# Expert blocks woven between the steps of a DFT token mixer, with weights fetched per block

## The chip, the cores and the metric

One core of one Trainium2 chip runs the kernel. The metric is device time in microseconds (us) of one execution; lower is better. All data are float32 except two small bfloat16 matrices used for counting. Engines: PE = TensorE, DVE = VectorE, ACT = ScalarE, POOL = GpSimd, SP = SyncE, which here only issues DMAs.

## What is computed

```python
X = np.fft.fft(np.fft.fft(x, axis=1), axis=2).real      # x: 8 batches x 2496 tokens x 256
x = X.reshape(19968, 256)
logits = x @ w_gate                                      # 8 experts
expert_idx = np.argmax(logits, axis=1)
gate_w = softmax(logits)[arange, expert_idx]
for e in range(8):                                       # rows of expert e
    y[e's rows] = relu(x[e's rows] @ w1[e]) @ w2[e]      # 256 -> 1024 -> 256
out = gate_w[:, None] * y
```

Each token goes to one expert; the number of tokens per expert is known only at run time.

## The kernel before

The work stands in two parts, one behind the other.

**The transform, batch by batch.** `first(b)` reads batch b in four quarters. A quarter is two DMAs, `xl` (SP queue, L192) and `xh` (POOL, an indirect DMA, L193), which `fold` adds and folds on DVE (L201 to L211). PE multiplies the result (tile `s`), ACT copies it to `t1` (L227), and SP writes it to a scratch tensor `Td` (L228). `xl` and `xh` have two buffers each. `second(b, h)`, for each half h of a batch, reads `Td` back in another layout (`t4`, printed as `t`, L242) and does five groups g: two small matmuls (tile `p`, from `m` and `t`), a copy to `z` on ACT, two matmuls with `rd` (tile `p`, 273 columns), and copies into `rows` on ACT (L260) and DVE (L261). Then `route` finds each token's expert on DVE, counts ranks on PE (tile `rk`, 11 small matmuls), and POOL scatters ten groups of 128 rows to `Xs` in DRAM, one indirect DMA each (L158). `Xs` has one region per expert. Two weight DMAs of 1 MB (L146, L148) per batch bring all eight experts into SBUF for good.

**The experts.** After the last batch, POOL writes 16 groups of padding rows, DVE makes a table `tab` (expert and first row of each of 85 blocks of 256 rows), and the block loop runs. `load` (SP) reads the block's 256 rows `xb`; `turn` copies the expert's first weights to `wc` (DVE) and transposes `xb` on PE (tile `pt`); `layer1` is 16 matmuls into four `ph` tiles, each evacuated with ReLU into `hT` by ACT (L416) or DVE (L414) in turn; `layer2` is 16 matmuls into one tile `py`, whose halves t = 0 and 1 are scaled by ACT into `y` (L428) and scattered by POOL to the output (L158). Every float32 matmul is two passes of PE in the trace. The loop calls `layer1(i + 1)` before `layer2(i)`. In the transform the order of instructions is chosen by a scheduler; in the block loop it is the order of the code. Each engine executes its own list strictly in that order, and so does each DMA queue's issuing engine.

Of the kernel before, what the change touches and what calls it, by code (L numbers as in the profile page):

```python
# [12 lines left out]
I32 = mybir.dt.int32  # L13
# [14 lines left out]
BLK = 256  # L28
CAP = NT + BLK
NBLK = (NT + E * (BLK - 1)) // BLK  # L30
# [17 lines left out]
def shape_consts():  # L48
    """Tables of the transform and of the token numbering; they depend on the shapes alone."""
# [59 lines left out]

def block_consts():  # L110
    c = {
        "i": np.arange(NBLK),
        "i256": BLK * np.arange(NBLK),
        "e9": np.arange(E + 1),
        "low": (np.arange(E)[None, :] <= np.arange(E)[:, None]).reshape(-1),
        "cap": CAP * np.arange(E),
    }
# [8 lines left out]
def kernel(ctx: ExitStack, tc, x, w_gate, w1, w2, out):  # L126
# [12 lines left out]
    wp = ctx.enter_context(tc.tile_pool(name="wp", bufs=1))  # L139
    w1_sb = wp.tile([128, E, 2 * F], F32, name="w1_sb")  # L140
    w2_sb = wp.tile([128, E, FC * D], F32, name="w2_sb")
    ident = wp.tile([128, 128], F32, name="ident")
    tab = wp.tile([1, 2, NBLK], I32, name="tab")

    def load_weights(e):
        nc.sync.dma_start(out=w1_sb[:, e].rearrange("p (c f) -> p c f", c=2),  # L146
                          in_=w1[e].rearrange("(c p) f -> p c f", p=128))
        nc.sync.dma_start(out=w2_sb[:, e].rearrange("p (c d) -> p c d", c=FC),  # L148
                          in_=w2[e].rearrange("(c p) d -> p c d", p=128))

    # rows of Xs are written once each, before any block reads them
    def unordered(ins, group):
        ins = getattr(ins, "ins", ins)
        tc.declare_no_dep(ins, group=group, reason="no row is written twice")
        tc.add_to_no_dep_group(group, ins)

    def put_row(dst, idx, rows, last, group):
        unordered(pool.indirect_dma_start(  # L158
# [4 lines left out]
    with ExitStack() as keep, ExitStack() as mix:  # L163
        cp = keep.enter_context(tc.tile_pool(name="cp", bufs=1))
        xp = mix.enter_context(tc.tile_pool(name="xp", bufs=2))
        sp = mix.enter_context(tc.tile_pool(name="sp", bufs=2))
        ps1 = mix.enter_context(tc.tile_pool(name="ps1", bufs=2, space=PSUM))
        ps2 = mix.enter_context(tc.tile_pool(name="ps2", bufs=2, space=PSUM))
        ps3 = mix.enter_context(tc.tile_pool(name="ps3", bufs=2, space=PSUM))
        psr = mix.enter_context(tc.tile_pool(name="psr", bufs=2, space=PSUM))  # L170

        ix = cp.tile([NA, B * 4], I32, name="ix")
        at = (np.arange(B)[:, None] * (S // 4) + 7 - np.arange(4))[None]
        at = (at + 8 * (NA - 1 - np.arange(NA))[:, None, None]).reshape(NA, B * 4)
        nc.sync.dma_start(out=ix[:], in_=const_dram("ix", at.astype(np.int32)))

        con = {}
        for n, v in shape_consts().items():
            wide = (128, 2, NY + 2 * E) if n == "rd" else v.shape
            con[n] = t = cp.tile(list(wide), F32, name=n)  # L180
            act.dma_start(out=t[:, :, 0:NY] if n == "rd" else t[:], in_=const_dram(n, v))
        wg = cp.tile([128, 2, E], F32, name="wg")
        act.dma_start(out=wg[:], in_=w_gate.rearrange("(c p) e -> p c e", p=128))
        act.dma_start(out=ident[:], in_=const_dram("ident", np.eye(128, dtype=np.float32)))

        xrows = x.rearrange("b (n j) d -> (b n) (j d)", j=4)

        def load_x(b, q):
            xl = xp.tile([NA, 4, D], F32, tag="xl", name="xl")
            xh = xp.tile([NA, 4, D], F32, tag="xh", name="xh")  # L190
            src = x[b].rearrange("(p j) d -> p j d", j=NB)
            nc.sync.dma_start(out=xl[:], in_=src[:, 4 * q + 1:4 * q + 5])  # L192
            pool.indirect_dma_start(  # L193
                out=xh[:].rearrange("p j d -> p (j d)"), out_offset=None, in_=xrows,
                in_offset=bass.IndirectOffsetOnAxis(ap=ix[:, 4 * b + q:4 * b + q + 1], axis=0))
            return xl, xh

        def fold_d(o, a, n):
            """o = [a[d] + a[-d] for d in 0..128 | a[d] - a[-d] for d in 1..127], a[0] and a[128] once."""
            lo, hi = free(a, 1, [D, n], [1, H - 1]), free(a, D - 1, [D, n], [-1, H - 1])  # L200
            vec.tensor_tensor(free(o, 1, [D, n], [1, H - 1]), lo, hi, op=ALU.add)  # L201
            vec.tensor_tensor(free(o, H + 1, [D, n], [1, H - 1]), lo, hi, op=ALU.subtract)
            vec.tensor_copy(free(o, 0, [D, n], [H, 2]), free(a, 0, [D, n], [H, 2]))

        def fold(xl, xh, q):
            """The sum of x[s, d] and x[-s, -d], folded over d, in place of xh."""
            n = 3 if q == 3 else 4
            a, m = xl[:], xh[:]
            vec.tensor_tensor(free(a, 1, [D, n], [1, D - 1]), free(a, 1, [D, n], [1, D - 1]),
                              free(m, 3 * D + D - 1, [-D, n], [-1, D - 1]), op=ALU.add)  # L210
            vec.tensor_tensor(free(a, 0, [D, n]), free(a, 0, [D, n]), free(m, 3 * D, [-D, n]), op=ALU.add)  # L211
            fold_d(m, a, 4)
            return xh

        def stage1(b, q, pm, pm0):
            t1 = xp.tile([NR, 4, D], F32, tag="t1", name="t1")
            for half in range(2):
                ps = ps1.tile([NR, 2, D], F32, tag="s1", name="s1")
                for i in range(2):
                    s = 4 * q + 2 * half + i  # L220
                    if s < 15:
                        mm(ps[:, i], con["w1"][:, s], pm[:, 2 * half + i])
                        continue
                    for k, lo, hi in ((15, 0, H + 1), (17, H + 1, D)):
                        mm(ps[:, i, lo:hi], con["w1"][:, k], pm0[:, lo:hi], True, False)
                        mm(ps[:, i, lo:hi], con["w1"][:, k + 1], pm[:, 3, lo:hi], False, True)
                act.copy(t1[:, 2 * half:2 * half + 2], ps[:])  # L227
            nc.sync.dma_start(out=Td[b][:, 4 * q * D:4 * (q + 1) * D], in_=t1[:].rearrange("p j d -> p (j d)"))  # L228

        def first(b):  # L230
            x0 = xp.tile([NA, D], F32, tag="x0", name="x0")
            nc.sync.dma_start(out=x0[:], in_=x[b].rearrange("(p j) d -> p j d", j=NB)[:, 0])
            pm0 = xp.tile([NA, D], F32, tag="pm0", name="pm0")
# [86 lines left out]
        for b in range(B):  # L320
            if b + 1 < B:
                first(b + 1)
# [145 lines left out]
```

## Time and profile before

| | |
|---|---|
| median of 3 runs | 1748.61 us (1746.11 to 1749.07) |
| profiled execution, span | 1751.1 us |
| PE busy | 1500.2 us (86% of the span) |
| DVE, ACT, POOL busy | 463.7, 283.4, 381.4 us |
| first pass of the experts starts | 460.79 us |
| DMA moved | 127.45 MB, mean 73 GB/s |

The profiled execution's span lies 2.5 us above the median of the runs; the page lists no other time for it. "Granted clock" (PEclk) is the share of TensorE's full 2.4 GHz; its two levels are 1.2 and 2.4 GHz, so 0.70 is a mixture of the two. In a row of the timeline the first two numbers are the start and the length in us, and `[8.85 <-DVE oh L280]` means that the engine stood idle for 8.85 us just before it, until DVE had written `oh`.

### The profile page before, as it was taken

How to read it: one execution, taken by the hardware profiler on the slowest of the kernel's cores; microseconds unless marked ns; L12 is line 12 of the kernel's file. 1: busy time of each engine (PE TensorE's matmuls, PEld its weight loads, DVE VectorE, ACT ScalarE, POOL GpSimd, SP SyncE). 2: the span in 40 equal slices, each digit the busy share in tenths (PEclk: the TensorE clock that was granted, in tenths of full speed). 3: DMA queues.
4: the chain of work that ended last, by engine and by line, in shares of the span. 5: the costliest groups of instructions: out<-in, count | busy, mean ns of one | idle time of the engine just before them, and what ended most of it. 6: DMA issues, size and time to landing. Idle time of an engine off the chain costs nothing.

```text
span 1751.1 us, 20321 instructions
## 1 busy us (share of the span) xinstructions
PE 1500.2 (86%) x6940; PEld 1258.7 (72%) x6940; DVE 463.7 (26%) x1084; ACT 283.4 (16%) x581; POOL 381.4 (22%) x382
## 2 busy tenths in 40 slices
PE   3667776652599999999999999999999999999998
PEld 2445554542488888888888888888888888888886
DVE  3444443423222122222222212222222222222220
ACT  1222222221011111111111111111111111111111
POOL 1155554556211111111111111111111111111111
PEclk9987766776699999999999999999999999999999
DMA  8777766632211111101111111110111111111100
GB/s 212 207 246 213 216 198 197 191 108 79 76 37 37 36 33 37 36 29 34 37 34 33 37 37 37 35 37 28 35 37 34 37 35 37 36 37 37 29 18 0
DMA packets 62977, 127.45 MB, mean 73 GB/s; under 512 B 11612, under 2 KB 31696, under 8 KB 62880
## 3 DMA queue, kind: packets, MB, share of 16 engines
q1 hardware_dynamic: 40323, 71.35, 14.6%
q0 software_dynamic: 20192, 53.43, 9.2%
q10 hardware_dynamic: 2365, 1.38, 0.4%
q8 instruction: 61, 1.00, 0.3%
q14 instruction: 36, 0.29, 0.1%
HBM read 72.19 MB, written 56.28 MB: 73 GB/s over the span
## 4 chain that ended last, share of the span: by engine, by line
issue 65%; POOL 10%; PE 2%; DMA 1%; POOLq 1%; DVE 1%; ACT 0%; SPq 0%; DVEq 0%; ACTq 0%
POOL out_dram L158 9%; PE p L131 1%; POOL Xs L158 1%; POOLq L158 1%; DMA Xs<-rows,pi 0%; DMA Xs<-pad,ti 0%; ACT z L256 0%; DMA xb<-Xs 0%; PE rk L131 0%; DVE rows L261 0%; PE pr L131 0%; POOLq L463 0%; DVE eq L274 0%; DVE mx L273 0%; DVE eq L275 0%
## 5 line engine op out<-in xcount | busy, mean ns | idle before, releaser
L131 PE MATMUL py<-w_sb,hT 128*128 x2720 | 623.5, 382 | 48.0 <-ACT y L428 48.0
L131 PEld LDWEIGHTS py<-w_sb,hT 128*128 128x128 f32 x2720 | 509.8, 190 | 148.1 <-ACT y L428 82.2
L131 PE MATMUL ph<-xT,wc 128*128 128x256 f32 x2720 | 603.0, 380 | 0.0
L131 PEld LDWEIGHTS ph<-xT,wc 128*128 128x128 f32 x2720 | 511.6, 191 | 66.5
L158 POOL DMA_INDIRECT out_dram<-y,ro x170 | 165.2, 971 | 1127.7 <-ACT y L428 1118.1
L414 DVE TENSOR_SCALAR hT<-ph 128x512 f32<-128x512 f32 x170 | 117.5, 691 | 476.9 <-PE ph L131 476.9
L428 ACT ACTIVATE y<-py,xb 128x256 f32<-128x256 f32 x170 | 80.5, 473 | 712.1 <-PE py L131 712.1
L400 DVE COPY xT<-pt 128x512 f32<-128x512 f32 x85 | 58.7, 691 | 500.0 <-PE pt L398 500.0
L158 POOL DMA_INDIRECT Xs<-rows,pi x160 | 167.1, 1044 | 83.0 <-issue 61.8
L416 ACT ACTIVATE hT<-ph 128x512 f32<-128x512 f32 x170 | 101.5, 597 | 434.0 <-PE ph L131 386.0
L131 PE MATMUL s<-xh,w 78*80 78x256 f32 (+2 forms) x272 | 89.1, 475 | 54.0 <-issue 18.9
L131 PE MATMUL p<-rd,z 128*128 128x273 f32 x320 | 110.8, 497 | 13.7 <-DVE lg L262 9.3
L392 DVE COPY wc<-w_sb 128x2048 f32 x85 | 104.3, 1227 | 38.7 <-DMA Xs<-pad,ti 30.2
L131 PEld LDWEIGHTS s<-xh,w 78*80 78x80 f32 x272 | 49.5, 196 | 79.5 <-issue 54.2
L131 PEld LDWEIGHTS p<-rd,z 128*128 128x128 f32 x320 | 71.4, 237 | 41.3 <-ACT z L256 15.0
L398 PE MATMUL pt<-ident,xb 128*128 128x128 f32 x340 | 52.0, 276 | 41.1 <-DVE ro L394 41.1
L398 PEld LDWEIGHTS pt<-ident,xb 128*128 128x128 f32 x340 | 43.0, 143 | 49.9 <-issue 41.2
L131 PE MATMUL rk<-oh,tri 128*128 128x88 bf16 x16 | 3.8, 236 | 83.2 <-DVE oh L280 83.2
L131 PEld LDWEIGHTS <-ones 128*128 128x128 bf16 x160 | 8.4, 121 | 86.7 <-issue 86.6
L193 POOL DMA_INDIRECT xh<-in_x_dram,ix x32 | 33.4, 1043 | 146.9 <-PE s L131 71.9
L131 PEld LDWEIGHTS p<-m,t 128*128 128x128 f32 x320 | 55.5, 238 | 7.8 <-DVE t L247 2.8
L131 PE MATMUL p<-m,t 128*128 128x128 f32 x320 | 57.6, 325 | 1.8 <-DVE t L247 1.8
(75 smaller groups left out, 388.5 us busy)
## 6 DMA issues: line engine op xcount, KB each, us to landing
xb<-Xs SPq DMA_DIRECT2D x85, 258.0 KB
w_sb<-in_moe_w_dram SPq DMA_DIRECT2D x16, 1024.0 KB
Td<-t SPq DMA_DIRECT2D x32, 320.0 KB
t<-Td SPq DMA_DIRECT2D x16, 640.0 KB
xl<-in_x_dram SPq DMA_DIRECT2D x32, 312.0 KB
out_dram<-y,ro POOLq DMA_INDIRECT x170, 2.8
Xs<-rows,pi POOLq DMA_INDIRECT x160, 5.7
x<-in_x_dram SPq DMA_DIRECT2D x8, 78.0 KB
```

The costliest lines, as they stand in the source:

```text
L131: nc.tensor.matmul(o, lhsT=lhsT, rhs=rhs, start=start, stop=stop)
L158: unordered(pool.indirect_dma_start(out=dst, out_offset=bass.IndirectOffsetOnAxis(ap=idx, axis=0), in_=rows, in_offset=None, bounds_check= ...
L193: pool.indirect_dma_start(out=xh[:].rearrange("p j d -> p (j d)"), out_offset=None, in_=xrows, in_offset=bass.IndirectOffsetOnAxis(ap=ix[: ...
L392: vec.tensor_copy(wc[:], w1_sb[:, ds(ev, 1)])
L398: nc.tensor.transpose(pt[:, c, t], xb[:, t, c * 128:(c + 1) * 128], ident[:])
L400: vec.tensor_copy(xT[:], pt[:].rearrange("p c t k -> p c (t k)"))
L414: vec.tensor_scalar(o, ph[:], 0.0, None, op0=ALU.max)
L416: act.activation(o, ph[:], ACTF.Relu)
L428: act.activation(y[:, t], py[:, t], ACTF.Copy, scale=xb[:, t, D + 1:D + 2])
```

## The change

The two parts are merged. A batch's tokens are worked on by the experts while the next batch is transformed.

- `rounds()` fixes, from shapes alone, how many blocks can surely be filled after each batch: 2 blocks of 256 rows after batch 0, 6 of 256 after batch 1, 3 of 512 after batch 2, 5 of 512 after each of batches 3 to 7, and then 21 of 256 for what is left. That is 57 blocks and 21,760 rows, the same number of rows as 85 blocks of 256. `plan` makes a table on DVE for each of these groups at run time.
- `first` and `second` become generators that stop after each small step. `mixed(b)` alternates the steps of `first(b + 1)` and `second(b)`, 26 stops, and ends with the plan. A step of `second` does the first matmuls of group g and the second matmuls of group g - 1.
- `experts(todo)` is a generator too; it stops after each `ph` tile (counted 1) and each `py` tile (counted 2), 16 counts for a block of 512. The main loop gives `mixed` a number of steps for each count, so that all steps of a batch are used up in about four tenths of the counts of the round beside it (27 calls at 42 per 0.6 of a round).
- A block fetches its own `xb`, `w1` (1 MB) and `w2` (1 MB) by three SP DMAs, one block ahead, with two buffers of each. The resident weights, the `wc` copy and the weight index on PE are gone.
- The whole program is in the order of the code. `layer1` and `layer2` of a block follow each other; `py` is one tile of 128 rows with its own buffer; `hT` and `xT` have one buffer; PSUM is shared by both parts (`pm_` 3, `pst` 1, `psh` 2, `psy` 2 buffers).

```diff
-NBLK = (NT + E * (BLK - 1)) // BLK
+BIG, BLK = 512, 256
+TICKS = 42
-    w1_sb = wp.tile([128, E, 2 * F], F32, name="w1_sb")
-    w2_sb = wp.tile([128, E, FC * D], F32, name="w2_sb")
+    def fetch(b, size, tab, i):
+        n = size // 128
+        row = nc.sync.value_load(tab[:, 0, i:i + 1], min_val=0, max_val=ROWS - size)
+        ev = nc.sync.value_load(tab[:, 1, i:i + 1], min_val=0, max_val=E - 1)
+        xb = bp.tile([128, BIG // 128, W], F32, tag="xb", name="xb")
+        taken(nc.sync.dma_start(out=xb[:, 0:n].rearrange("p t c -> p (t c)"),
+                                in_=Xs[ds(row, size)].rearrange("(p t) c -> p (t c)", t=n)), b)
+        w1_sb = bp.tile([128, 2, F], F32, tag="w1", name="w1_sb")
+        nc.sync.dma_start(out=w1_sb[:], in_=w1[ds(ev, 1)].rearrange("o (c p) f -> p (o c) f", p=128))
+        w2_sb = bp.tile([128, FC, D], F32, tag="w2", name="w2_sb")
+        nc.sync.dma_start(out=w2_sb[:], in_=w2[ds(ev, 1)].rearrange("o (c p) d -> p (o c) d", p=128))
...
+            for f in range(FC // m):
+                ph = psh.tile([128, m, size], F32, tag="h", name="ph")
...
+                yield 1
+            if follow:
+                while follow[:3] not in tabs:
+                    yield 0
+                got = got or fetch_next()
+                turned = turn(follow[1], got[0])
+            y = bp.tile([128, BIG // 128, D], F32, tag="y", name="y")
+            for i in range(n):
+                py = psy.tile([128, D], F32, tag="y", name="py")
+                for f in range(FC):
+                    mm(py[:], hT[:, f, i * 128:(i + 1) * 128], w2_sb[:, f], f == 0, f == FC - 1)
+                act.activation(y[:, i], py[:], ACTF.Copy, scale=xb[:, i, D + 1:D + 2])
+                put_row(out, ro[:, i:i + 1], y[:, i], NT - 1, "out")
+                if i < n - 1 or n == 2:
+                    xT = next(turned, xT)
+                yield 2
...
+    for b in range(1, B):
+        side, done, due = mixed(b), 0, 0.0
+        total = 16 * sum(k * size for size, k, _ in rounds()[b - 1]) / BIG
+        while done < total:
+            w = next(work)
+            done += w
+            due += TICKS * w / (0.6 * total) if w else 1
+            while due >= 1:
+                next(side, None)
+                due -= 1
+        for _ in side:
+            pass
+    for _ in work:
+        pass
```

Where instructions stand on PE. Before, in the block loop (`pt` transposes, `ph` layer 1, then the reading of the expert's number and the first matmul of layer 2):

```order
L398 MATMUL pt<-ident,xb 128x128 x4
L131 MATMUL ph<-xT,wc 128x256 x16
L421 TENSOR_LOAD tab
L421 ISA x2
L131 ISA
L131 MATMUL py<-w_sb,hT 128x256
```

Now, in a block of 512 rows of the fifth round (`pr`, `p`, `s` are the transform's, `t_2600` a half of its batch):

```order
L162 MATMUL ph<-xT,w_sb 128x512 x10
L162 MATMUL pr<-t_2600,rot 128x5
L162 MATMUL ph<-xT,w_sb 128x512 x2
L162 MATMUL p_2914<-m_84,t_2600 128x128 x2
L162 MATMUL ph<-xT,w_sb 128x512 x2
L162 MATMUL p_2924<-m_84,t_2600 128x128 x2
L162 MATMUL p_2929<-rd,z 128x273 x2
L162 MATMUL ph<-xT,w_sb 128x512 x2
L162 MATMUL p_2939<-m_84,t_2600 128x128 x2
L162 MATMUL p_2944<-rd,z 128x273 x2
L162 MATMUL s_2951<-xh,w_82 80x256 x2
L162 MATMUL py<-w_sb,hT 128x256 x8
```

The transform's matmuls stand one step at a time between the block's, and no block starts with a reading of a number on PE any more.

On DVE, in the block loop before, one block (with what each instruction waits for):

```order
L392 COPY wc<-w_sb 128x2048 [waits DVE_49]
L394 CAST ro<-xb 128x2 [waits DMAHW0_49,DMASW3_49,DMASW2_49]
L400 COPY xT<-pt 128x512 [waits DVE_49,PE_49]
L414 TENSOR_SCALAR hT<-ph 128x512 [waits DVE_49,PE_49,Activation_49]
L414 TENSOR_SCALAR hT<-ph 128x512 [waits PE_49]
```

Now, in the same block of the fifth round:

```order
L490 TENSOR_SCALAR hT<-ph 128x512 [waits PE_49]
L240 TENSOR_TENSOR xl<-xl,xh 78x4x255 [waits DMAHW3_49,DMASW1_49]
L326 COPY rows<-p_2929 128x256 [waits DMASW4_49,DMASW5_49,DMASW2_49,DMASW7_49,DMASW0_49,Activation_49]
L327 COPY lg<-p_2929 128x16
L490 TENSOR_SCALAR hT<-ph 128x512 [waits PE_49]
```

A fold of the transform (L240), which waits for the two DMAs of its quarter, stands between two evacuations of the same block.

On SP, before, each block (a reading of its first row, and one DMA):

```order
L382 TENSOR_LOAD tab
L382 ISA x2
L384 ISA
L384 DMA xb<-Xs 128x516
```

Now, with a fetch of a block and what follows it in the fourth round:

```order
L439 DMA xb<-Xs 128x1032
L442 ISA
L442 DMA w_sb<-in_moe_w_dram 128x2x1024
L444 ISA
L444 DMA w_sb<-in_moe_w_dram 128x8x256
L298 DMA t_2139<-Td 128x5x256
L288 DMA Td<-t_2182 80x1024
L223 DMA xl<-in_x_dram 78x1024
```

The transform's reads and writes stand behind the two weight DMAs of a block on the same queue.

## Rows read from the trace of the kernel before

**Rows 1.** The page: PE's busy tenths and its granted clock in 40 slices.

```profile
PE   3667776652599999999999999999999999999998
PEclk9987766776699999999999999999999999999999
```

**Rows 2.** Busy time by stretch; then clock, DMA share, GB/s. Transform, then experts.

```profile
300.00:325.00 25.00, 17.48 (x72) 12.79 (x72) 10.85 (x39) 6.84 (x17) 14.03 (x13) 0.70 0.72 206
...
475.00:1735.00 1260.00, 1212.57 (x5677) 1041.06 (x5676) 279.06 (x413) 178.76 (x334) 162.24 (x167) 1.00 0.11 34
```

**Rows 3.** Timeline of PE: the start of the experts, and one later block.

```profile
460.79 1.57 PE L131 MATMUL ph<-xT,wc 128*128 128x256 f32 x3
...
1004.86 3.62 PE L131 MATMUL py<-w_sb,hT 128*128 x16
1009.04 3.72 PE L131 MATMUL py<-w_sb,hT 128*128 x16 [0.56 <-ACT y L428]
1012.60 0.60 PE L398 MATMUL pt<-ident,xb 128*128 128x128 f32 x4
1013.04 7.07 PE L131 MATMUL ph<-xT,wc 128*128 128x256 f32 x32
1019.95 3.62 PE L131 MATMUL py<-w_sb,hT 128*128 x16
...
1740.44 3.72 PE L131 MATMUL py<-w_sb,hT 128*128 x16 [0.61 <-ACT y L428]
```

**Rows 4.** Timeline of PE in the transform's second stage, at both clocks.

```profile
74.12 0.43 PE L131 MATMUL pr<-t,rot 128*128 128x5 f32 x2
74.41 2.06 PE L131 MATMUL p<-m,t 128*128 128x128 f32 x8
...
80.62 2.11 PE L131 MATMUL p<-rd,z 128*128 128x273 f32 x8
82.57 0.83 PE L131 MATMUL p<-m,t 128*128 128x128 f32 x6
...
84.94 3.22 PE L131 MATMUL s<-xh,w 78*80 78x256 f32 x14
88.00 0.20 PE L131 MATMUL rk<-oh,tri 128*128 128x88 bf16 x1
...
89.14 0.71 PE L131 MATMUL p<-m,t 128*128 128x128 f32 x4 [0.46 <-DVE t L247]
...
111.02 0.23 PE L131 MATMUL rk<-oh,tri 128*128 128x88 bf16 x1 [8.85 <-DVE oh L280]
```

**Rows 5.** Timeline of ACT and POOL: batch 0's last copy; scatters of batches 0 and 1.

```profile
42.71 0.58 ACT L227 COPY t<-s 80x512 f32<-80x512 f32 x1 [1.94 <-PE s L131]
...
90.34 1.01 POOL L158 DMA_INDIRECT Xs<-rows,pi  x1 [0.93 <-ACT z L256]
...
104.24 0.98 POOL L193 DMA_INDIRECT xh<-in_x_dram,ix  x1 [0.31 <-issue]
...
114.21 1.18 POOL L158 DMA_INDIRECT Xs<-rows,pi  x1 [0.32 <-issue]
...
159.42 1.19 POOL L158 DMA_INDIRECT Xs<-rows,pi  x1 [0.32 <-issue]
```

**Rows 6.** Between the parts: the last landing (chain); SP's first block loads.

```profile
452.10 3.12 DMA Xs<-pad,ti
455.67 45.10 SPq L384 DMA_DIRECT2D xb<-Xs  x8
```

**Rows 7.** Issue to landing of `xh` (L193), in us.

```profile
DMA to landing us min/median/max: 4.5/7.9/11.9
```

**Rows 8.** A weight DMA (L148) on SP; stretches with full and idle DMA engines.

```profile
11.74 0.40 SPq L148 DMA_DIRECT2D w_sb<-in_moe_w_dram  x1
4.00:20.00 16.00, 3.45 (x8) 1.89 (x8) 5.97 (x14) 0.00 (x0) 2.09 (x2) 1.00 1.02 260
375.00:400.00 25.00, 11.52 (x56) 9.01 (x55) 5.63 (x30) 4.36 (x12) 12.67 (x14) 0.79 0.29 103
```

More of the change, by code (lines that the diff above doesn't have):

```diff
@@ L155, in unordered @@
         tc.add_to_no_dep_group(group, ins)
+        return ins
     def put_row(dst, idx, rows, last, group):
-        unordered(pool.indirect_dma_start(
+        return unordered(pool.indirect_dma_start(
             out=dst, out_offset=bass.IndirectOffsetOnAxis(ap=idx, axis=0),
             in_=rows, in_offset=None, bounds_check=last, oob_is_err=False), group)
[L163 to L230, printed above, removed]
@@ new lines, in sent, with taken @@
+    def sent(ins, b):
+        tc.declare_no_dep(ins, group="taken", reason="no block before this batch's round has these rows")
+        tc.add_to_no_dep_group(f"xs{b}", ins)
+    def taken(ins, b):
+        ins = getattr(ins, "ins", ins)
+        if b + 1 < B:
+            tc.declare_no_dep(ins, group=f"xs{b + 1}", reason="a block has rows of its round's batches alone")
+        tc.add_to_no_dep_group("taken", ins)
+    cp = ctx.enter_context(tc.tile_pool(name="cp", bufs=1))
+    xp = ctx.enter_context(tc.tile_pool(name="xp", bufs=2))
@@ new lines, in first @@
+    def first(b):
+        x0 = ahead.pop((b, "x0"))
+        pm0 = xp.tile([NA, D], F32, tag="pm0", name="pm0")
+        fold_d(pm0[:], x0[:], 1)
+        for q in range(5):
+            f = iter(())
+            if q < 4:
+                xl, xh = ahead.pop((b, q))
+                f = fold(xl, xh, q)
+            next(f, None)
+            yield
+            if q:
+                t1 = xp.tile([NR, 4, D], F32, tag="t1", name="t1")
+                half1(b, q - 1, 0, pm, pm0, t1)
+            next(f, None)
+            yield
+            if q:
+                half1(b, q - 1, 1, pm, pm0, t1)
+                nc.sync.dma_start(out=Td[b][:, 4 * (q - 1) * D:4 * q * D], in_=t1[:].rearrange("p j d -> p (j d)"))
+                load(b + (q + 1) // 4, (q + 1) % 4)
+            next(f, None)
+            pm = xh
+            yield
@@ L431, with mixed @@
-    for i in range(4):
-        load(i)
-    turn(0)
-    turn(1)
-    layer1(0)
-    for i in range(NBLK):
-        if i + 4 < NBLK:
-            load(i + 4)
-        if i + 2 < NBLK:
-            turn(i + 2)
-        if i + 1 < NBLK:
-            layer1(i + 1)
-        layer2(i)
+                sent(put_row(Xs, ti[:, e, k:k + 1], pad[:], ROWS - 1, "xs"), b)
+    def mixed(b):
+        one, two = (first(b + 1) if b + 1 < B else iter(())), second(b)
+        for _ in range(3):
+            next(one, None)
+            yield
+        regroup(b, 1)
+        for k, _ in enumerate(two):
+            if k % 2:
+                next(one, None)
+            yield
+        for _ in one:
+            yield
+        if b + 1 < B:
+            regroup(b + 1, 0)
+        else:
+            pads(b)
+        for size, k, last in rounds()[b]:
+            tabs[b, size, last] = plan(size, k, last)
@@ new lines @@
+    load(0, 0)
+    load(0, 1)
+    for _ in first(0):
+        pass
+    regroup(0, 0)
+    for _ in mixed(0):
+        pass
+    work = experts(todo)
+    for b in range(1, B):
[9 more added lines that the diff above has]
+        for _ in side:
+            pass
@@ L446 @@
+    for _ in work:
+        pass
 _INS = ["x", "moe_w_gate", "moe_w1", "moe_w2"]
```

431 lines of the change are left out of this document (252 added, 179 removed).

## Prediction

> **What bounds the kernel now.** I read the page's slices first. PE is at 9 from slice 12 on and at 5 to 7 before that, and its granted clock is 0.9 or 1.0 against 0.6 to 0.7 [rows 1]. So there are two regimes. The table of stretches says the same in numbers: in the expert part PE is busy 1212.57 of 1260 us at clock 1.00 with the DMA engines 0.11 busy; in 25 us of the transform PE is busy 17.48 us at clock 0.70, with the DMA engines 0.72 busy [rows 2]. The expert part is bound by PE, the transform by chains of small steps: in the timeline PE waits 8.85 us for `oh` there, in one piece [rows 4]. The first pass of the experts is at 460.79 us, the last `py` ends at 1744.16 us (1740.44 + 3.72) [rows 3]. So 461 us of the span hold little PE work, and 1283 us hold 85 blocks at 15.09 us (1004.86 to 1019.95) [rows 3].
>
> **The sum after the change** has six terms; everything below is one core's time along PE's list, because PE is the engine that nearly all later waits end at.
>
> 1. Start, to the first expert pass. Nothing is woven yet. Batch 0's last stage-one copy ends at 43.3 us (42.71 + 0.58) [rows 5]. Then `Td` is written and read back, two landings: the trace shows 3.12 us for one when the queues are empty and 7.9 us for `xh` in traffic [rows 6, 7]; I take 4 each, since no weights are loaded at this point any more, 8 us. From `pr` to the first scatter is 16.2 us (74.12 to 90.34), to the second half's first scatter 23.9 us more (90.34 to 114.21), ten scatters take 13.9 us (90.34 to 104.24) [rows 4, 5]. The last lands in 3.1 us, and from SP's first block load to the first expert pass are 5.1 us (455.67 to 460.79) [rows 3, 6]; `w1` behind it adds about 1.5. Sum 43.3 + 8 + 16.2 + 23.9 + 13.9 + 3.1 + 5.1 + 1.5 = **115 us**. Bounds 100 (the first half of `second` runs without `first` beside it) and 130 (both landings at 7.9, and steps in a fixed order).
>
> 2. The first round: two blocks of 256 beside all steps of `second(1)` and `first(2)`. A batch took 45.2 us before (114.21 to 159.42) [rows 5]; PE's idle 30% of it (7.5 of 25 us [rows 2]) is 13.6 us, room for most of one block. The second block ends only after the next plan's first `xb` has come, since its transposes stand inside it: 2.3 us from `rk` to the first scatter (88.00 to 90.34 [rows 4, 5]), then 13.9 + 3.1 + 5.1, and half of its layer 2, 3.6 us. 45.2 + 2.3 + 22.1 + 3.6, rounded up for the rest of block 0: **75 us**; bounds 60 and 95.
>
> 3. The other 83 blocks' worth of rows (21,760 rows are 85 times 256, two are done). Of 15.09 us per block, 0.56 is the wait for ACT's `y` between the two halves of one `py` tile, with 0.06 for refilling: 4.18 us from start to start against 3.56 for the other half [rows 3]. With one `py` tile per half and two buffers that wait goes; what is late next is the next pass itself. 32 passes of layer 1 take 6.91 us from start to start (1013.04 to 1019.95), 0.216 each, so 64 are 13.8, and the transposes 0.44 (1012.60 to 1013.04): 14.25 us [rows 3]. Blocks of 512 columns pay the same per column. 83 x 14.25 = **1183 us**; bounds 83 x 14.1 = 1170 and, if the wait came back in another form (layer 2 now follows its own layer 1 and needs its last evacuation in its seventh and eighth matmul, 2.6 us in), 83 x 15.09 = 1252.
>
> 4. The transform's own PE time in rounds 2 to 7, at the full clock. Per batch: 40 passes of `p<-m` at 0.83/6 = 0.138, 5.5 us; 40 of `p<-rd` at (82.57 - 80.62)/8 = 0.244, 9.8; 30 wide passes of `s` at (88.00 - 84.94)/14 = 0.219 and 8 half-wide at about 0.11, 7.4; `rk` and `pr` 1.1 twice (88.00 to 89.14), 2.3 [rows 4]. About 24 us with the fills overlapped by the block's passes. Five rounds have both generators, the last only `second`, 17 us: 5 x 24 + 17 = **137 us**. At the lower clock a pass takes twice as long: eight `p<-m` took 2.06 us at 74.41, six 0.83 at 82.57 [rows 4].
>
> 5. New waits. The fold's first instruction waits for `xh`, and evacuations of the block stand behind it on DVE; PE can fill two `ph` tiles, 3.5 us, before it stands too. `xh` takes 4.5 to 11.9 us to land [rows 7], and is issued two steps before its use (27 steps lie in four tenths of a round's 85 or 143 us and 24 us of their own, 2.1 or 3 us a step), on POOL behind up to ten scatters of 1.3 us; `xl` stands on SP behind 2 MB of weights. The nearest row for what PE loses by that is the 8.85 us wait for `oh`, which I put down to the same cause [rows 4]. I take one such wait per batch in rounds 2 to 6: **44 us**; bounds 0 (it falls into layer 2, which needs DVE little) and two per batch, 88.
>
> 6. The end: from the last `py` pass to the end of the span 6.9 us (1744.16 to 1751.1) [rows 3], **7 us**, unchanged.
>
> Sum 115 + 75 + 1183 + 137 + 44 + 7 = 1561 us of span, 190 less than the 1751.1 of the profiled execution. That one lies 2.5 us above the median of the runs, so I predict 1558 us for the median.
>
> Edits put at nothing: the `wc` copies on DVE, hidden before under PE. The plans, about 20 small DVE instructions per round, run while `ph` tiles are in reserve; uncovered, 3 us per round. The padding scatters, 16 x 1.3 us with nothing beside them before, now lie beside round 7's first half, whose blocks need POOL only for outputs. And the weight fetch, 2 MB per block, 57 times, against 2 MB per expert once: a fetch has one block, 14.25 us or more, to land. A block of 256 moves 2.10 MB of weights, 0.26 of rows in and 0.26 out, 2.62 MB, which needs 184 GB/s. With weights, constants and batch 0 on the way, the engines moved 260 GB/s at share 1.02 [rows 8]; so 10 us, hidden with 4 us to spare.
>
> Here the Trainium skill speaks against the change: Perfetto Trace Analysis, section DMA Optimizations, says that small DMAs, under 2 KB, carry a significant overhead per transfer, and `w2` comes in runs of 1 KB. The trace's answer is that the `w2` load at 11.74 us, in the same runs, lay in the stretch that reached 260 GB/s [rows 8]. By the rule the last rival below would be likelier; by the row it isn't.
>
> **Rivals.**
> - *The weave is smoother than I think.* No waits of term 5, start and first round at their lower bounds: 1561 - 44 - 15 - 15 = 1487, less 2.5, about 1485. For it: the steps are software-pipelined, and before, PE had an idle third to wait in anyway. Against it: the fold's wait stands in the list [rows 7].
> - *The weave stalls, and the clock falls with it.* In rounds 2 to 7 side steps cost what a batch cost before, 45.2 us, instead of 24 + 8.85: 5 x 12 and some 20 in the last, +80; and the experts' passes inside those four tenths, about 50 us a round, run at granted clock 0.70 as in the transform [rows 2], x 0.43 = 21 us in each of six rounds, but only as far as the waits recur, say half, +60. 1561 + 140, about 1700. For it: the clock was at 0.70 wherever PE waited. Against it: with expert passes in reserve PE stands far less. The Trainium skill, TensorE: Matmul & The Clock Gate, section "Loop structure matters more than you think", warns of just this, DMA waits between groups of matmuls; that the clock falls behind such waits the trace shows (0.70 [rows 2]).
> - *The weights don't come in time: slower than before.* One mechanism, in the 21 blocks of 256 at the end and the six of round 2: block time becomes 2.62 MB over the rate reached. It decides below 184 GB/s. At 117 GB/s a block takes 22.4 us, 21 x 8.2 + 6 x 4 = 196 us are added, and the gain is gone; at 103 GB/s it is 25.4 us, 21 x 11.2 + 6 x 7 + some 30 in the big blocks = 307, 1865 us. For it: the 103 GB/s that the trace shows late in the transform. Against it: there the engines were only 0.29 busy, so nothing asked for more [rows 8].
> - That the change doesn't weave at all is excluded by PE's list in the section on the change.
>
> **How the numbers follow.** My forecast, near 1558 (1495 to 1640): 0.72. Smoother, below 1495: 0.09. Stalls with the clock, 1640 to 1740: 0.13. Late weights: 0.05, almost all of it above 1750. Some mixture that ends within 0.2% of before, which is about what a measurement of this kernel can tell from no change: 0.01. Faster is 0.72 + 0.09 + 0.13 = 0.94, same 0.01, slower 0.05. The range: below 1495 lies 0.09, above 1640 a good 0.1 (most of the stalls, and late weights) once the upper bounds of terms 2, 3 and 5 are taken in; so 1495 to 1640.
>
> **What would show it.** Right: first expert pass near 115 us, granted clock 1.00 from round 2 on, `ph` passes every 0.216 us in the last 300 us, a block there in 14.25 us, PE's idle time in rounds 2 to 6 behind DVE's fold and about 9 us a batch. Wrong: PE waiting for a weight DMA at the head of a block; a block in the last 300 us above 15 us; clock below 0.9 beside blocks of 512; a first expert pass later than 130 us.

## The result and the profile after

The changed kernel took 1582.8 us (median of 4 runs, 1578.2 to 1588.0) against 1748.8 us for the kernel before (1746.1 to 1749.6): a ratio of 0.905, 95% interval 0.903 to 0.907. 1558 us were predicted, in a range of 1495 to 1640. The profiled execution shown here has a span of 1576.4 us, against the 1751.1 us of before.

First the page of the changed kernel: PE's busy tenths and its granted clock in 40 slices of 39.4 us, and its line of totals, which answer to [rows 1].

```profile
PE 1441.3 (91%) x6044; PEld 1074.1 (68%) x6044; DVE 387.8 (25%) x1130; ACT 281.3 (18%) x581; POOL 371.4 (24%) x382
...
PE   2546897997998999989998999999999999999998
...
PEclk9867798998999999999999999999999999999999
```

Before, PE was below 9 in the first eleven slices of 43.8 us, and at 9 after that (the last is at 8). Now it is below 9 in the first five (197 us), and later only in single slices: the 7th and the 10th are at 7, the 13th, 18th and 22nd at 8, and so is the last. The clock is below 0.9 in the 2nd to 5th slice, and in the 7th and 10th. So the two regimes are gone, and what is left to explain are a start of five slices and a series of dents.

The timeline of PE shows the marks that the prediction's terms speak of: the first expert pass (`ph`), the second round's first one, and two blocks at the end. Columns are start, busy time, engine, line, operation, tiles, shape, count, and in brackets the idle time before and what ended it.

```profile
121.96 1.12 PE L454 MATMUL pt<-ident,xb 128*128 128x128 f32 x4 [16.75 <-DMA xb<-Xs]
126.06 3.75 PE L162 MATMUL ph<-xT,w_sb 128*128 128x256 f32 x8 [2.99 <-DMA w_sb<-in_moe_w_dram]
...
205.62 1.75 PE L162 MATMUL ph<-xT,w_sb 128*128 128x256 f32 x7 [0.27 <-DMA w_sb<-in_moe_w_dram]
...
1541.34 7.07 PE L162 MATMUL ph<-xT,w_sb 128*128 128x256 f32 x32
1548.25 3.62 PE L162 MATMUL py<-w_sb,hT 128*128 128x256 f32 x16
1551.70 0.60 PE L454 MATMUL pt<-ident,xb 128*128 128x128 f32 x4
1552.14 3.62 PE L162 MATMUL py<-w_sb,hT 128*128 128x256 f32 x16
1555.59 7.07 PE L162 MATMUL ph<-xT,w_sb 128*128 128x256 f32 x32
1562.50 7.07 PE L162 MATMUL py<-w_sb,hT 128*128 128x256 f32 x32
```

A block of 256 rows takes 14.25 us (1541.34 to 1555.59), with no idle time in brackets; before it was 15.09 with 0.56 us behind ACT's `y` [rows 3]. The last pass ends at 1569.57 us (1562.50 + 7.07).

The dents: DVE in rounds 3 and 4, then PE at the same places, then the stretches around the first of them (busy time of PE, PEld, DVE, ACT, POOL; granted clock, DMA share, GB/s).

```profile
381.77 0.95 DVE L240 TENSOR_TENSOR xl<-xl,xh 78x765 f32<-78x765 f32 x1 [13.46 <-DMA xh<-in_x_dram,ix]
...
511.29 0.95 DVE L240 TENSOR_TENSOR xl<-xl,xh 78x765 f32<-78x765 f32 x1 [9.22 <-DMA xh<-in_x_dram,ix]
...
383.19 1.23 PE L162 MATMUL p<-m,t 128*128 128x128 f32 x4 [8.77 <-DVE lg L327]
...
512.75 1.96 PE L162 MATMUL s<-xh,w 78*80 78x256 f32 x4 [5.46 <-issue]
...
350.00:375.00 25.00, 23.58 (x124) 18.82 (x122) 9.00 (x32) 7.38 (x18) 11.08 (x11) 1.00 0.38 111
375.00:400.00 25.00, 15.10 (x67) 10.77 (x68) 9.64 (x42) 4.15 (x10) 9.34 (x10) 0.80 0.38 97
400.00:425.00 25.00, 25.00 (x97) 17.50 (x96) 5.62 (x17) 3.79 (x8) 10.24 (x11) 1.00 0.65 221
```

The fold's first instruction (L240) stands at the head of DVE's list until `xh` has landed. `rows` and `lg`, which free PE's tiles, stand behind it, so PE stops 8.77 and 5.46 us, and in the stretch with the longer stop the granted clock is 0.80. That happens once a batch, five times in rounds 2 to 6 (4.68, 8.77, 5.46, 5.01 and 5.11 us, 29 us together); from 225 us on PE's idle time is 40 us in all. Two more folds wait so before the second round, at 93.99 and 171.16 us.

Why `xh` lands so late is seen on POOL, which issues it:

```profile
375.15 0.97 POOL L177 DMA_INDIRECT Xs<-rows,pi  x1 [0.30 <-issue]
376.43 0.97 POOL L177 DMA_INDIRECT Xs<-rows,pi  x1 [0.30 <-issue]
377.71 0.98 POOL L224 DMA_INDIRECT xh<-in_x_dram,ix  x1 [0.31 <-issue]
```

The load of the fourth quarter is the next instruction behind a row of scatters, 1.28 us each, and goes out at 377.71; the transfer itself takes 4.0 us from there.

### The profile page after: what moved, and what is told of

Same layout as the page of the kernel before. It is cut to its first block, busy times and chain, and to the rows that moved or that the text cites. A ratio compares the mean times of both kernels' runs of the same rounds, so it can differ in the third digit from the quotient of the medians.

```text
span 1576.4 us, 16703 instructions
## 1 busy us (share of the span) xinstructions
PE 1441.3 (91%) x6044; PEld 1074.1 (68%) x6044; DVE 387.8 (25%) x1130; ACT 281.3 (18%) x581; POOL 371.4 (24%) x382
## 2 busy tenths in 40 slices
DMA packets 123218, 229.98 MB, mean 146 GB/s; under 512 B 12733, under 2 KB 82992, under 8 KB 123136
## 4 chain that ended last, share of the span: by engine, by line
PE 50%; issue 31%; POOL 6%; DMA 3%; DVE 1%; POOLq 0%; ACT 0%; SPq 0%; DVEq 0%; ACTq 0%
PE ph L162 21%; PE py L162 19%; PE p L162 6%; POOL out_dram L177 5%; PE s L162 2%; POOL Xs L177 2%; PE pt L454 1%; DMA w_sb<-in_moe_w_dram 1%; DMA xl<-in_x_dram 1%; DMA xh<-in_x_dram,ix 1%; DMA Xs<-rows,pi 1%; DVE xl L240 0%; POOLq L177 0%; PE rk L162 0%; DVE xT L455 0%
## 5 line engine op out<-in xcount | busy, mean ns | idle before, releaser
L162 PE MATMUL ph<-xT,w_sb 128*128 128x256 f32 (+1 forms) x1824 | 611.8, 490 | 4.7 <-DMA w_sb<-in_moe_w_dram 3.3
L162 PE MATMUL py<-w_sb,hT 128*128 128x256 f32 x2720 | 615.6, 381 | 0.0
L162 PEld LDWEIGHTS ph<-xT,w_sb 128*128 128x128 f32 x1824 | 348.6, 192 | 217.3 <-issue 182.9
L177 POOL DMA_INDIRECT Xs<-rows,pi x160 | 158.5, 991 | 99.3 <-issue 53.4
L162 PE MATMUL s<-xh,w 78*80 78x256 f32 (+2 forms) x272 | 84.3, 443 | 35.5 <-issue 15.6
L162 PE MATMUL p<-rd,z 128*128 128x273 f32 x320 | 95.4, 425 | 7.6 <-DVE lg L327 6.9
L162 PEld LDWEIGHTS p<-rd,z 128*128 128x128 f32 x320 | 61.1, 208 | 19.6 <-DVE lg L327 7.4
L240 DVE TENSOR_TENSOR xl<-xl,xh 78x1020 f32<-78x1020 f32 (+1 forms) x32 | 36.7, 1147 | 113.3 <-DMA xh<-in_x_dram,ix 73.4
L326 DVE COPY rows<-p 128x256 f32<-128x256 f32 x80 | 33.8, 423 | 110.3 <-ACT rows L325 110.3
L257 ACT COPY t<-s 80x512 f32<-80x512 f32 x64 | 37.1, 580 | 85.4 <-PE s L162 85.4
```

Of the source, the lines that this page charges most:

```text
L162: nc.tensor.matmul(o, lhsT=lhsT, rhs=rhs, start=start, stop=stop)
L177: return unordered(pool.indirect_dma_start(out=dst, out_offset=bass.IndirectOffsetOnAxis(ap=idx, axis=0), in_=rows, in_offset=None, bounds ...
L326: vec.tensor_copy(rows[:, k + 1, 0:D], free(p3[:], D, [-1, D]))
```

## The experiments

The kernels ran in sets, each beside the kernel before on one chip. The sets fell on different chips, and on two of these something shows in the traces that is absent on the others: increments of the engines' semaphores, the counters by which one engine tells another that a result is ready, that come late (last section). A comparison is therefore made inside a set, or between sets without late increments. These are the sets of `ctl_after` and of `both2`, and the runs of the result above.

### One part alone: a `py` tile per half (b_pysplit)

```diff
-        py = psy.tile([128, 2, D], F32, tag="y", name="py")
         for t in range(2):
+            py = psy.tile([128, D], F32, tag="y", name="py")
...
-            act.activation(y[:, t], py[:, t], ACTF.Copy, scale=xb[:, t, D + 1:D + 2])
+            act.activation(y[:, t], py[:], ACTF.Copy, scale=xb[:, t, D + 1:D + 2])
```

> The kernel before, with one part of the change alone: layer 2 has a py tile of its own for each half of a block, not one tile for both. Theory (the 0.56-us wait for ACT's y between the halves, with its refill, is the only thing that the blocks lose): a block takes 14.25 us in place of 15.09, 85 blocks give 71 us, the time is about 1678 us. Rival A (the wait only moves, because ACT's evacuation of the first half then stands in front of the next block): block 14.6 to 15.1, 1710 to 1749 us. Rival B (the gain of the change in the blocks needs the order of the change, layer 1 directly ahead of its own layer 2): no change, 1749 us.

Measured: 1680.6 us against 1753.6 in its set, ratio 0.959 (0.957 to 0.962), 73 us less. PE's timeline of a late block of this kernel:

```profile
1002.90 7.07 PE L131 MATMUL py<-w_sb,hT 128*128 x32
1009.80 0.60 PE L398 MATMUL pt<-ident,xb 128*128 128x128 f32 x4
1010.24 7.07 PE L131 MATMUL ph<-xT,wc 128*128 128x256 f32 x32
1017.15 3.19 PE L131 MATMUL py<-w_sb,hT 128*128 x14
```

From `py` to `py` 14.25 us, and no wait in brackets where 0.56 stood [rows 3]. The theory holds to 2 us: 85 blocks times 0.84 are 71. Late increments stand in this trace too, but the first expert pass is at 459.73 us (460.79 before), so the gain lies in the blocks. So 73 us, as against 166 for the whole change, come from one edit that has nothing to do with the weaving.

### The fold's waits for `xh` and `xl` (a_xbuf, xbuf2, with ctl_after)

```diff
-        xl = xp.tile([NA, 4, D], F32, tag="xl", name="xl")
-        xh = xp.tile([NA, 4, D], F32, tag="xh", name="xh")
+        xl = xp.tile([NA, 4, D], F32, tag="xl", name="xl", bufs=3)
+        xh = xp.tile([NA, 4, D], F32, tag="xh", name="xh", bufs=3)
...
-                load(b + (q + 1) // 4, (q + 1) % 4)
+                load(b + (q + 2) // 4, (q + 2) % 4)
...
     load(0, 1)
+    load(0, 2)
```

> The changed kernel with three buffers for xl and xh instead of two, and each quarter's loads issued one quarter earlier. Theory (the five stalls of PE of 4.7 to 10 us in rounds 2 to 6, one per batch, come from the fold of the fourth quarter that waits for xh to land): DVE's waits for xh fall from 73 us to under 15, the stalls of PE go, the span falls by 35 to 40 us, and the granted clock stays at 1.00 behind the places where it fell to 0.80 to 0.86. Rival A (what is late next is xl or DVE's queue itself): stalls shrink by less than half, under 15 us gained. Rival B (the earlier loads, on POOL's and SP's queues, hold up the scatters and the blocks' own loads): no gain, or up to 20 us slower.

Measured: 1592.2 us, which is 9 us more than the changed kernel had taken elsewhere. But this run has late increments, and its waits stand at places where no program of the set waits otherwise ("remote" is the profile's word for a release that it can't put down to an instruction). So the same kernel was run again, with the changed kernel itself beside it.

> The changed kernel itself, run again beside its variants, so that they are compared on one chip. In the first four variants, increments of the engines' semaphores reach their waiters up to 15 us late wherever POOL issues a row of scatters; the traces of the kernel before and of the changed kernel show no such case. Theory (that is a property of where those variants ran): the changed kernel shows it too here, and takes 1600 to 1640 us. Rival (it is a property of the variants): 1578 to 1588 us as before, no late increment.

Measured: 1583.8 us (1582.7 to 1584.0), ratio 0.9055 to a before of 1751.5, no late increment. The number is the rival's, and the result above is reproduced. The rival's reason is not borne out: the two variants that had late increments before have none beside it (`xbuf2`, `nofetch2`). So late increments belong to the set in which a kernel runs and not to the kernel; whether to its chip or to something else of that set, these runs don't tell apart.

> The variant with three buffers for xl and xh and loads one quarter earlier, again, now beside the changed kernel. It took 1592 us, with next to no wait for xh left, but stalls at new places behind late semaphore increments. Theory (fold waits for xh are the changed kernel's stalls): 30 to 40 us below the changed kernel in this set. Rival (removing one wait only uncovers the next): within 15 us of it.

Measured: 1501.0 us (1499.0 to 1502.7), ratio 0.858 (0.855 to 0.861) to before, 82.7 us below the changed kernel beside it. From the table of waits (total us, times, longest), first of `ctl_after`:

```profile
DVE xl L240 <- DMA xh<-in_x_dram,ix: 74.0, 7, 13.5
...
DVE xl L240 <- DMA xl<-in_x_dram: 39.8, 10, 8.8
...
POOL Xs L177 <- DVE xl L243: 26.7, 6, 11.0
```

and of `xbuf2`:

```profile
DVE xl L240 <- DMA xh<-in_x_dram,ix: 5.7, 1, 5.7
...
DVE xl L240 <- DMA xl<-in_x_dram: 0.9, 1, 0.9
...
POOL Xs L177 <- DVE xl L243: 13.8, 3, 6.3
```

The page of `xbuf2` has PE at 9 from the 6th slice on, and the clock at 0.9 from the 5th:

```profile
PE 1418.2 (95%) x6044; PEld 1062.5 (71%) x6044; DVE 389.6 (26%) x1130; ACT 281.3 (19%) x581; POOL 372.0 (25%) x382
...
PE   3639899999999999999999999999999999999998
...
PEclk9968999999999999999999999999999999999999
```

The cause was right, but I had put its size at half of what it is. The edit takes away `xl`'s waits with `xh`'s, so the 82.7 us are the price of both; no run parts them. The marks of the rounds, read from PE's `ph` passes, tell where the 81 us between the two spans (1582.0 and 1500.7) lie:

```
first pass of          ctl_after   xbuf2    stage, ctl_after / xbuf2
round 1                126.7       109.7    126.7 / 109.7
round 2                206.6       178.4     79.9 /  68.7
blocks of 512          334.3       290.5    127.7 / 112.1
last blocks of 256    1276.1      1194.8    941.9 / 904.3
last py pass          1574.8      1493.4    298.6 / 298.6
```

53 us (15.6 + 37.6) lie in rounds 2 to 7, where I had looked: PE's idle time there falls from 40.0 to 5.8 us, 34 us, and its busy time from 1328.9 to 1309.6 us, 19 us, since passes behind a stop ran at a lower clock. Another 28 us lie ahead of round 2: 17 before the first expert pass, where the fold of batch 1 holds up batch 0's scatters, and 11 in round 1. In the changed kernel's trace of the result above, POOL waited 10.44 us there, behind a fold that had waited for `xl`, and the next fold waited for `xh`:

```profile
72.59 1.22 DVE L240 TENSOR_TENSOR xl<-xl,xh 78x1020 f32<-78x1020 f32 x1 [4.06 <-DMA xl<-in_x_dram]
93.99 0.95 DVE L240 TENSOR_TENSOR xl<-xl,xh 78x765 f32<-78x765 f32 x1 [12.09 <-DMA xh<-in_x_dram,ix]
...
76.77 1.37 POOL L177 DMA_INDIRECT Xs<-rows,pi  x1 [10.44 <-DVE xl L243]
...
103.05 1.02 POOL L177 DMA_INDIRECT Xs<-rows,pi  x1 [2.47 <-issue]
```

In `xbuf2` the same first scatter is at 70.95 us, and the second half's scatters are over by 99.5.

### Do the weights cost anything? (a_nofetch, nofetch2, fetch2)

```diff
+        if held:
+            return (xb, *held)
...
-        w1_sb = bp.tile([128, 2, F], F32, tag="w1", name="w1_sb")
+        w1_sb = cp.tile([128, 2, F], F32, name="w1_sb")
...
-        w2_sb = bp.tile([128, FC, D], F32, tag="w2", name="w2_sb")
+        w2_sb = cp.tile([128, FC, D], F32, name="w2_sb")
...
+        held.extend([w1_sb, w2_sb])
```

> The changed kernel, but the weights are fetched for the first block alone and kept; every block then multiplies by the first block's weights, so this part of the computation is changed. 56 fetches of 2 MB, 119 MB of 230, are left out. Theory (the per-block weights land in time and cost nothing but 3 us at the first block of each of two rounds): 1570 to 1583 us, a block at the end still 14.25 us. Rival (weights on the DMA queues are what makes xh and xl land late, so the fetches cost PE the stalls of rounds 2 to 6): the waits for xh fall from 9 us to 4 to 5, and the time falls by 20 to 40 us, to 1543 to 1563.

Measured: 1639.3 us, outside of what either theory allowed, in the set with late increments. Run again beside the changed kernel:

> The variant that keeps the first block's weights for all blocks (its products are changed by that), again, now beside the changed kernel. It took 1639 us where the changed kernel was not beside it. Theory (weight fetches cost PE next to nothing, and the 1639 us came from late semaphore increments): within 15 us of the changed kernel in this set. Rival A (weights on the queues make xh and xl late): 20 to 40 us below it. Rival B (without the weight loads the order of the queues changes and the scatters run into the blocks): 40 to 60 us above it, as 1639 stands to 1583.

Measured: 1581.2 us (1579.8 to 1582.8) against 1583.8 for the changed kernel. Half of all bytes are gone (112.51 MB in place of 229.98), and DVE's wait for `xh` is 72.5 us against 74.0, for `xl` 39.6 against 39.8. The theory holds: the weights neither cost PE time that shows nor make `xh` or `xl` late. For `xh` its place on POOL's list does (377.71 us, above); why `xl` is late was not looked into.

```diff
+        for n2, src in (("w1x", w1), ("w2x", w2)):
+            wx = bp.tile([128, FC * D], F32, tag=n2, name="wx")
+            c = 2 if n2 == "w1x" else FC
+            nc.sync.dma_start(out=wx[:].rearrange("p (c f) -> p c f", c=c), in_=src[ds(ev, 1)].rearrange("o (c p) f -> p (o c) f", p=128))
         w1_sb = bp.tile([128, 2, F], F32, tag="w1", name="w1_sb")
```

> The changed kernel, where every block fetches both weights twice, the first time into tiles that nothing reads, ahead of the real ones: 4.7 MB for a block of 256 in place of 2.6. Theory (the transfers are hidden only as long as a block's bytes land within its 14.25 us, so there is a margin of 14.25 to about 10 us, and beyond it the block takes bytes over the rate reached, 260 GB/s at most): a block of 256 takes about 18 us, 21 of them at the end and six in round 2 add 80 to 110 us, blocks of 512 stay as they are. Rival (the rate reached is lower than 260 GB/s, near the 200 of the last stretch, so the change ran close to its limit): a block takes 23 us and more, over 200 us are added. Rival B (two fetches fit as well): under 20 us.

Measured: 1586.5 us (1585.0 to 1594.5), 2.8 us more than the changed kernel; rival B. (The execution profiled here was the slowest of its five, 1594.5 us.) A stretch of the last blocks, and one block of it on PE:

```profile
1500.00:1525.00 25.00, 25.00 (x120) 22.03 (x119) 3.53 (x6) 3.81 (x7) 2.91 (x3) 1.00 0.91 325
...
1500.60 7.07 PE L162 MATMUL ph<-xT,w_sb 128*128 128x256 f32 x32
...
1514.85 7.07 PE L162 MATMUL ph<-xT,w_sb 128*128 128x256 f32 x32
```

The block still takes 14.25 us, while the DMA engines move 325 GB/s at share 0.91. My 260 GB/s [rows 8] was what one mix of transfers reached at the start, not what the queues can do; 4.72 MB in 14.25 us need 331 GB/s, and they get it. So the change could fetch twice its weights. It was not free everywhere: PE waits 8.32, 6.61 and 4.22 us for weights at the heads of three of the first eight blocks (at 133.93, 219.19 and 319.77 us), where `ctl_after` has one such wait of 2.70 us. By the share of 0.91 the limit is likely near, but it was not reached. The Trainium skill warns in Perfetto Trace Analysis, section DMA Optimizations, of the overhead of transfers under 2 KB; the page of this run has 143184 of 198005 packets under 2 KB, and the row above shows what they reach all the same.

### What the weaving is worth (a_serial, serial2)

```diff
         total = 16 * sum(k * size for size, k, _ in rounds()[b - 1]) / BIG
+        for _ in side:
+            pass
```

(and a third buffer for the plan's small tables, which this order needs.)

> The changed kernel without the weaving: all steps of a round's transform are issued ahead of the round's blocks, everything else (block sizes, weights per block, the plan per round) stays. Theory (most of the gain is that the transform's 45 us a batch lie beside expert work, 24 us of it PE's own): each of rounds 1 to 6 pays some 20 to 25 us of PE's idle time more and its transform's passes at the lower clock, together 120 to 190 us, so 1700 to 1770 us, and PE's busy share is 5 to 7 tenths again in the stretches of the transform. Rival (the gain is mostly from faster blocks and the shorter end, the weaving itself is worth little): under 60 us slower than the changed kernel, below 1640 us.

Measured: 1709.5 us, ratio 0.976 (0.973 to 0.980). The set has late increments, so it was run once more:

> The changed kernel without the weaving (all steps of a round's transform ahead of the round's blocks), again. It took 1709 us where increments of the engines' semaphores came late. Theory (the overlap is worth most of the gain): in rounds 1 to 6 PE's list has 45 us of transform per batch in which PE is busy 5 to 7 tenths at the lower clock, in place of 24 us of passes and 6 us of stall: 15 to 20 us in each of six rounds, so 90 to 125 us above the changed kernel's 1583: 1673 to 1708. Rival (the 1709 us came from late increments, and the weaving is worth little): under 1640.

Measured: 1711.2 us (1708.4 to 1719.0), with late increments again. PE in two neighbouring stretches of round 5 of `serial2`, one with blocks and one with the bare transform:

```profile
850.00:875.00 25.00, 25.00 (x88) 16.01 (x88) 3.88 (x7) 3.97 (x8) 3.88 (x4) 1.00 0.44 153
...
900.00:925.00 25.00, 14.60 (x61) 10.90 (x61) 5.82 (x24) 5.25 (x13) 11.15 (x11) 0.73 0.38 111
```

14.60 of 25 us at clock 0.73: that is much like [rows 2] again. The number has to be set against kernels that ran with late increments too. The changed kernel itself did not, but two variants that differ from it little did: 1639.3 (`a_nofetch`) and 1642.4 (`head`, below). Against these the order without weaving costs about 70 us. Without late increments it is at most 1711 - 1584 = 127 us, if they cost this kernel nothing. What they cost it can be estimated from PE's timeline of `serial2`, where three stops stand behind an instruction of DVE that the profile calls released from "remote":

```profile
280.93 2.07 PE L162 MATMUL py<-w_sb,hT 128*128 128x256 f32 x4 [3.27 <-DVE hT L490]
...
1131.12 0.70 PE L162 MATMUL py<-w_sb,hT 128*128 128x256 f32 x2 [3.06 <-DVE hT L490]
...
1146.74 1.11 PE L454 MATMUL pt<-ident,xb 128*128 128x128 f32 x4 [7.56 <-DVE xT L455]
```

These are 14 us, and with smaller waits beside them and one of 5.84 us for `oh` (0.87 to 0.97 in the other batches) some 25. By that estimate the weaving is worth about 100 us, inside the theory's 90 to 125; the rival's under 1640 us would need late increments to cost 71 us here. The pair was not run without them.

In the first set three kernels stand side by side: 1753.6 before, 1680.6 with the `py` tiles alone, 1709.5 with everything but the weaving. So the rest of the change (loads, plans and blocks round by round, without weaving) loses some 29 us there, late increments included, and the weaving has to earn them first. That `py` and the weaving add up to the whole gain is therefore not shown to the microsecond.

### A head start for the first block (head, both, both2)

```diff
                 got = fetch(b, size, tabs[b, size, last], at)
+                yield 0
                 for xT in turn(size, got[0]):
...
+        if b == 1:
+            next(work)
+            for _ in range(8):
+                next(side, None)
```

> The changed kernel with a head start in round 1: the first block's load is issued, then eight of the transform's steps, and only then its transposes, so that the 16 us wait for xb and the 3 us wait for the weights at the first block are filled with work. Theory (these waits are lost time): 10 to 18 us below the changed kernel, 1565 to 1573. Rival (the steps only move; the second block of round 1 waits for the next plan's rows at the same time as before, which sets the round's end): within 4 us.

Measured: 1642.4 us, with late increments and no changed kernel beside it: it says nothing on its own theory.

> Three buffers for xl and xh with loads one quarter earlier, and the head start in round 1, together. With the loads alone it took 1501 us. Theory (the waits at the first block, 18 us there, are filled): 1483 to 1493. Rival (the round's end is set by the transform's chain, not by the first block's start): 1497 to 1503.

Measured: 1594.7 us (1592.4 to 1600.0), with late increments; `a_xbuf` took 1592.2 with them.

> Three buffers with earlier loads and the head start in round 1, once more. With late increments of the engines' semaphores the pair took 1594 us and the loads alone 1592; without them the loads alone took 1501. Theory (the head start is worth the 9 us by which round 3 began earlier, and late increments are a property of where a kernel runs): without late increments 1487 to 1497; with them 1590 to 1600 again. Rival (the head start's gain is given back later, whatever the increments do): 1499 to 1505 without them.

Measured: 1493.9 us (1492.0 to 1495.1), ratio 0.854 (0.852 to 0.856) to before, without late increments. The wait for `xb` at the first block, 16.75 us in the changed kernel, is 1.27 here:

```profile
108.13 0.66 PE L454 MATMUL pt<-ident,xb 128*128 128x128 f32 x4 [1.27 <-DMA xb<-Xs]
112.53 3.75 PE L162 MATMUL ph<-xT,w_sb 128*128 128x256 f32 x8 [3.74 <-DMA w_sb<-in_moe_w_dram]
```

The first pass is no earlier than in `xbuf2` (112.5 against 109.7), but the blocks of 512 begin at 284.6 in place of 290.5, and the end is 7.5 us earlier. The median is 7 us lower and inside the theory's range, but the two kernels stood in two sets, whose kernels before differ by 2 us. This is the best kernel of the study: 89 us below the changed one, though measured in another set.

## Why the prediction was right, point by point

By its own terms, in the profiled execution:

1. *First expert pass*, 115 us predicted, 126.1 measured. Inside the bounds (100 to 130), 11 us over. `pr` came at 55.37 in place of 51.3: PE stood 10.81 us for `Td`, where I had put 8 for both landings, and the last copy came 1.9 us later. From there to the first scatter are 21.4 us, not 16.2, and on to the second half's first scatter 26.3, not 23.9 (76.77 and 103.05, shown above). So the mis-sized steps are "from `pr` to the first scatter" and "to the second half's": I had them from places of the kernel before, and allowed for no fold that waits ahead of them on DVE's list. In `xbuf2` the first of them takes 17.8 us, and the first pass is at 109.7.
2. *Round 1*, 75 predicted, 79.5 measured (126.06 to 205.62). PE stops 5.88 us at 173.18 here, behind the fold that waits for `xh` until 171.16; term 2 had no such stop, and `xbuf2` needs 68.7 us.
3. *The blocks*. 14.25 us for 256 rows, as predicted, and 28.42 for 512 (DVE's first evacuation of one block at 744.73, of the next at 773.15). 27 of the first kind and 28 of the second are 27 x 14.25 + 28 x 28.42 = 1181 us; 1183 were predicted. The time of a block was right, one part of its account not: 0.56 us of wait and 0.06 of refilling are 0.62, and 0.84 us went (`b_pysplit`).
4. and 5. *The transform's own time and the new waits*. From 205.62 to the last pass's end at 1569.57 are 1364 us, and the sum of terms 3 to 5 was 1364. Less the blocks, 183 us are left for 137 + 44 = 181. `xbuf2`, with next to no stop, needs 1315 us from 178.4 to its last pass's end at 1493.8, and 1315 - 1181 leave 134 for term 4, 6 us of idle time in them. The other 49 are term 5: 34 us more idle time of PE and 15 us of longer passes (1324.5 us busy against 1309.6). One wait per batch in rounds 2 to 6 was right in place (the fold's wait for `xh`) and count. Its size was not: the five stops are 29 us and not 44 (8.85 each). Smaller waits and the passes at a lower clock, which term 5 had not priced, made up the rest, so that its sum came out is in part luck.
6. *The end*, 7 us predicted, 6.8 measured.

Then the median lies 6.4 us above the profiled execution's span, where I had put it 2.5 below; the profiled execution was the fastest of the four. These 9 us, with 11 and 4.5 of terms 1 and 2, are all of the 25 between 1558 and 1583.

The rivals. *Smoother* (1485) did not happen here, but without the folds' waits the time comes near it: 1501. What I gave as 44 us is 83 when it is taken away, since the same waits also stand in terms 1 and 2 and lower the clock. *Stalls and the clock* happened in small: 0.80 in the worst stretch, then 1.00 again; I had priced 0.70 [rows 2] in four tenths of each round, for half of that time. The Trainium skill's warning that I set beside it (TensorE: Matmul & The Clock Gate, "Loop structure matters more than you think") points the right way: the dips of the clock lie exactly where PE waits between groups of passes, and passes took 15 us longer beside 34 us of idle time. *Late weights* stayed far off: twice the bytes cost 2.8 us. The two waits for weights at a block's head, 3.0 and 0.3 us, are at the first blocks of rounds 1 and 2, when nothing could be fetched ahead. The chances that I gave above 1640 sum to 0.19 (0.13, 0.05 and 0.01), where the text on the range says a good 0.1.

Of what should have shown it wrong, two came in part: PE waited for a weight DMA at the head of two blocks, those just named, and the clock was below 0.9 beside blocks of 512, in the stretches with a stop alone. The first pass at 126 us came near the 130 named.

## What to carry to other kernels

When two streams of work are woven into one list per engine, look at the first instruction of each step that waits for a DMA: all that stands behind it on that engine waits too, and the engine that pays is a third one. Give such loads one more buffer and issue them a step earlier, ahead of the rows of scatters on the same queue; here that was worth 83 us, as much as half of the change. And price a shared output tile by itself: a tile for each half gave 73 us in the kernel before. The woven blocks take the same 14.25 us, but the shared tile was not tried in them.

## What the runs showed of the hardware

**Late increments.** In two of the sets ACT and DVE stood idle with their input ready, up to 17 us. In `a_serial`, ACT, DVE and PE around one such place:

```profile
1119.52 0.60 PE L454 MATMUL pt<-ident,xb 128*128 128x128 f32 x4
1119.96 3.40 PE L162 MATMUL py<-w_sb,hT 128*128 128x256 f32 x15
1124.88 0.38 PE L162 MATMUL py<-w_sb,hT 128*128 128x256 f32 x1 [1.52 <-issue]
1137.68 1.11 PE L454 MATMUL pt<-ident,xb 128*128 128x128 f32 x4 [12.42 <-DVE xT L455]
...
1136.93 0.69 DVE L455 COPY xT<-pt 128x512 f32<-128x512 f32 x1 [18.37 <-remote]
...
1136.87 0.84 ACT L504 ACTIVATE y<-py,xb 128x256 f32<-128x256 f32 x2 [21.72 <-remote]
...
1132.20 0.98 POOL L177 DMA_INDIRECT Xs<-pad,ti  x1 [0.30 <-issue]
```

`xT` waits for PE's transposes alone, and these were over at 1120.1; the copy began at 1136.93, in the same moment as ACT's `y`, soon after the last of 26 scatters in a row (1132.20). In the trace's semaphore updates, PE's own counter does not move between 1117.85 and 1135.41 us, although passes that increment it began at 1118.44, 1118.87, 1119.31 and 1119.85. In seven of the traces (`b_pysplit`, `a_xbuf`, `a_serial`, `a_nofetch`, `serial2`, `head`, `both`) PE, ACT and DVE have 166 to 205 updates fewer than instructions that make one (2252 for 2425 in `a_serial`). Every instruction without an update within 0.5 us of its end ended within 13 us of a scatter to `Xs`. In the traces of before, after, and the other five, none lacks its update. What makes the difference was not found.

It costs a woven kernel much, and the kernel before little. The kernel with more buffers took 1592 us with late increments and 1501 without, the one without weight fetches 1639 and 1581, the last one 1595 and 1494; the kernel before took 1753.6 and 1756.8 in sets with them, 1749.4 and 1751.5 in sets without. A likely reason, not tested: before, scatters in rows are issued only in the transform, where PE waits anyway; woven, they run beside the blocks. So in such a set the change likely gains less: `a_nofetch`, which equals the changed kernel to 3 us elsewhere, has a ratio of 0.934 there, not 0.905. The changed kernel itself was not run in one.

**The DMA engines** moved 325 GB/s at share 0.91 with nearly three in four of that run's packets under 2 KB, a quarter more than the 260 GB/s at share 1.02 that I had taken for their limit [rows 8].
